# The branch between the two courses ahead of the rows' transposition, and three shared two-bank PSUM tiles

## The chip, the cores and the metric

The kernel runs on one core of one Trainium2 chip. The metric is the device time of one execution in microseconds; the median of three runs before the change is 544.16 us (542.45 to 544.39).

## The reference

Three layers follow each other. Everything is float32.

```python
scores = cap * np.tanh(scale * np.matmul(q, k.transpose(0, 1, 3, 2)) / cap)   # 2 x 12 heads, 448 x 64
attn = softmax(scores); x = (attn @ v) laid out as 896 tokens x 768
# mixture of experts: 8 experts, one for each token
expert_idx = np.argmax(logits, axis=1); gate_w = probs[np.arange(N), expert_idx]
for e in range(E):
    mask = expert_idx == e
    h = np.maximum(x[mask] @ w1[e], 0.0)          # 768 -> 1024
    out[mask] = gate_w[mask, None] * (h @ w2[e])  # 1024 -> 768
# feed-forward layer
r = np.maximum(x @ w_in, 0.0)                     # 768 -> 2048
return (s * (r * r) + b) @ w_out                  # 2048 -> 768
```

## The kernel before

The five engines each have a queue of instructions of their own: PE (matmuls), ACT, DVE and POOL (element-wise work; POOL also issues the indirect transfers) and SP (weight loads). The program runs in stages.

- **Attention**, to about 118 us, then **routing**, to about 130 us: DVE finds each token's expert and sorts the tokens by expert into slots. `rare` (L556) is a single flag made on the chip: it is 1 only where the experts' sizes don't fit the plan of two wide experts and six narrow ones. For the data that is timed it is 0.
- **Rows.** POOL gathers the sorted tokens, 128 at a time, with seven indirect transfers (L559). `rows(j)` (L652) transposes block j: six passes on PE into a PSUM tile `xt`, from which ACT copies the high part `xs0` (L668) and DVE the low part `xs1` (L669). For blocks 0 to 3 the gate is folded into the pass (L664); blocks 4 to 6 are gated on ACT first (L649) and go through a plain transposition (L662). The tiles `xt` come from the pool `ps_x`, three tiles of two banks.
- **Weights.** A matmul in float32 is made of three passes over a high and a low part (`mm3`, L638 to L641). `split` makes the parts: ACT casts the high one (L622), DVE or POOL subtracts (L623). `split1("R0", 0, pool)` and `split2("R0", 0, pool)` make the first parts of each layer, w10 and w20, with the subtraction on POOL.
- **Experts and feed-forward** are in `rest(fast)`, written once and called twice: `rest(True)` under `tc.If(rare_v < 1)` (L1044) is the fast course, `rest(False)` under `tc.If(rare_v > 0)` (L1050) the general one, with the experts' sizes in registers. Each engine loads `rare` into its sequencer (L833) and branches for itself.

Ahead of the first branch stand all seven blocks of rows, the first hidden block of the first wide expert (`layer1(0, S, 0, 0, hn)`, L710 and L712), the splits for it and for w20, and POOL's memsets (L830, L832). In `rest`, PE goes on with hidden block 1 (`hw`, L639 to L641, from w11) and the first sums `y` (from w20 and hh0), and then with the narrow experts, whose tokens DVE adds up at L771.

The sums stand in six PSUM tiles of one bank each (`accs`, tags y0 to y5, in the pool `ps_y`, which is opened after `ps_x` is closed). The last part of the feed-forward layer goes twice over half of the columns: seven sums (six tiles of `accs` and one of `ps_h`), each left by `leave(p, j)`, in which ACT (j even, L685) or DVE (j odd, L687) copies it and POOL stores it (L1011). At the end of the first half each sum gets three more passes and is left; at the end of the second half nine passes and is left. SP, PE, ACT and DVE go here in the order of the code.

Between tiles the framework sets semaphores: a write waits for what reads the tile that it overwrites, by tile. At an `If`, an engine that doesn't run a course raises the semaphores by what that course would have added; SP does this for the queues of the weight loads, after a wait for the loads that it has already issued, and POOL for the gathers.

Of the kernel before, what the change touches and what calls it, by code (L numbers as in the profile page):

```python
# [9 lines left out]
F32 = mybir.dt.float32  # L10
# [6 lines left out]
PSUM = bass.MemoryType.PSUM  # L17
# [4 lines left out]
B, H, S, D = 2, 12, 448, 64  # L22
NT = B * S
# [16 lines left out]
KD = DM // 128  # L40
NS = NT // 128
NPAD = NT + 224
# [17 lines left out]
def tile_kernel(ctx, tc, qk, vp, emb, scal, wp, wi, wo, out, dbg=None):  # L60
    nc = tc.nc
    pe, dve, act, pool, sp = nc.tensor, nc.vector, nc.scalar, nc.gpsimd, nc.sync
# [44 lines left out]
    def tabv(row, r, hi, engines=CORE):  # L107
        return nc.values_load(tab[0:1, row, r:r + 1], engines=engines, min_val=0, max_val=hi,
                              skip_runtime_bounds_check_because="made on chip from counts of tokens and one-hot rows")
# [17 lines left out]
    def done(*keys):  # L127
        for key in keys:
            used[key] = len(used)
# [25 lines left out]
    for i in range(1, 2 * NF1 + 1):  # L155
        c = i % 2
# [320 lines left out]
    xs = [big.tile([128, KD, NPAD], F32R, tag=f"a{i}", name=f"xs{i}") for i in range(2)]  # L477
# [3 lines left out]
    xctx2 = ExitStack()  # L481
    ps_x = xctx2.enter_context(tc.tile_pool(name="ps_x", bufs=3, space=PSUM, reuse_waits="tile"))
# [16 lines left out]
    def warm(n):  # L499

        t = ps_x.tile([128, 2, 512], F32, tag="xt", name="warm")
        for _ in range(n):
            pe.matmul(out=t[:, 0, 0:128], lhsT=ident, rhs=ident)
# [80 lines left out]
    dve.tensor_tensor(out=rv[:, 0], in0=rm, in1=bc(iota8[0:1], E, 1), op=ALU.mult)  # L584
    dve.tensor_reduce(out=gs, in_=gv.rearrange("p k j -> p j k"), axis=AX.X, op=ALU.add)

    warm(6)

    dgs = const.tile([128, GATES.count("p") * 128], F32, name="dgs")
    dg = {j: dgs[:, j * 128:(j + 1) * 128] for j in range(NS) if GATES[j] == "p"}  # L590
# [30 lines left out]
    def split(src, w, lo=dve):  # L621
        act.copy(out=w[0], in_=src)  # L622
        lo.tensor_tensor(out=w[1], in0=src, in1=w[0], op=ALU.subtract)  # L623

    def split1(u, f, lo=dve):
        key = (u, 0, f // 2)
        src = raw_t[key].rearrange("p (q k c j) -> p c k q j", q=4, k=KD, c=2)[:, f % 2]
        split(src, [t.rearrange("p k (q j) -> p k q j", q=4) for t in W1[f % 2]], lo)
        if f % 2:
            done(key)  # L630

    def split2(u, f, lo=dve):
        key = (u, 1, f // 2)
        split(raw_t[key].rearrange("p (c k f) -> p c k f", c=2, k=KD)[:, f % 2], W2[f % 2], lo)
        if f % 2:
            done(key)

    def mm3(out, ah, al, bh, bl, start, stop, **kw):  # L638
        pe.matmul(out=out, lhsT=ah, rhs=bh, start=start, stop=False, **kw)  # L639
        pe.matmul(out=out, lhsT=ah, rhs=bl, start=False, stop=False, **kw)  # L640
        pe.matmul(out=out, lhsT=al, rhs=bh, start=False, stop=stop, **kw)  # L641

    pump()
    rows_in.clear()
    split1("R0", 0, pool)

    def gate(j):
        if j < NS and GATES[j] == "a":
            act.mul(out=xg_t[j], in_=xg_t[j], mul=gs[:, j:j + 1])  # L649

    def rows(j):
        xg = xg_t[j]  # L652
        cs = slice(j * 128, (j + 1) * 128)

        n = 1 if j != 3 else 2
        ts = [ps_x.tile([128, 2, 512], F32, tag="xt", name="xt")[:, 0:2 // n, 0:384].rearrange("p a (k c) -> p a k c", k=3)
              for _ in range(n)]
        for kd in range(KD):
            o = ts[kd * n // KD][:, kd // 3 if n == 1 else 0, kd % 3]
            xr = xg[:, kd * 128:(kd + 1) * 128]  # L660
            if GATES[j] != "p":
                pe.transpose(out=o, in_=xr, identity=ident)  # L662
            else:
                pe.matmul(out=o, lhsT=xr, rhs=dg[j])  # L664
        for a, t in enumerate(ts):
            ks = slice(a * KD // n, (a + 1) * KD // n)
            xh, xl = (xs[i][:, ks, cs].rearrange("p (a k) c -> p a k c", k=3) for i in range(2))
            act.copy(out=xh, in_=t)  # L668
            dve.tensor_tensor(out=xl, in0=t, in1=xh, op=ALU.subtract)  # L669

    gate(0)
    gate(1)
    for j in range(4):
        if j < 2:
            gate(j + 2)
        rows(j)

    for j in range(4, NS):
        gate(j)
    hw = ps_h.tile([128, 512], F32, tag="h0", name="hw")  # L680
    hn = ps_h.tile([128, 512], F32, tag="h1", name="hn")

# [5 lines left out]


    def accs():  # L690
        return [ps_y.tile([128, 512], F32, tag=f"y{k}", name=f"y{k}") for k in range(KD)]

    def at(o, n):
        return slice(o, o + n) if isinstance(o, int) else bass.ds(o, n)

    def within(o, low):
        if isinstance(o, int):
            return o
        return nc.s_assert_within(o, 0, NT - low - 1, skip_runtime_bounds_check_because="the expert has more tokens here")

    def layer1(f, n, low, o, hw=hw):


        o = within(o, low)
        wh, wl = W1[f % 2]
        if f == 0 and hw is hn:

            for k in range(KD):
                for w in (wh, wl):
                    pe.matmul(out=hw[:, 0:n], lhsT=w[:, k], rhs=xs[0][:, k, at(o, n)], start=(k == 0 and w is wh), stop=False)  # L710
            for k in range(KD):
                pe.matmul(out=hw[:, 0:n], lhsT=wh[:, k], rhs=xs[1][:, k, at(o, n)], start=False, stop=(k == KD - 1))  # L712
        else:
            for k in range(KD):
                mm3(hw[:, 0:n], wh[:, k], wl[:, k], xs[0][:, k, at(o, n)], xs[1][:, k, at(o, n)], k == 0, k == KD - 1)
        hh, hl = (t[:, 0:n] for t in H2[f % 2])
        act.activation(out=hh, in_=hw[:, 0:n], func=ACTF.Relu)
        dve.scalar_tensor_tensor(out=hl, in0=hw[:, 0:n], scalar=0.0, in1=hh, op0=ALU.max, op1=ALU.subtract)
# [99 lines left out]


    y = [t.rearrange("p (k t) -> p k t", k=KD // 2) for t in (mem_y[:, 0:KD // 2 * NPAD], mem_y[:, KD // 2 * NPAD:])]  # L820

    split1("R0", 1)
    split2("R0", 0, pool)
    layer1(0, S, 0, 0, hn)
    for j in range(4, NS):
        rows(j)
    xctx2.close()
    ps_y = ctx.enter_context(tc.tile_pool(name="ps_y", bufs=1, space=PSUM, reuse_waits="tile"))
    for t in xs:
        pool.memset(t[:, :, NT:NPAD].bitcast(F32), 0.0)  # L830
    for t in y:
        pool.memset(t, 0.0)  # L832
    rare_v = nc.values_load(rare, engines=[ENG.SP, ENG.Pool] + CORE, min_val=0, max_val=1,  # L833
                            skip_runtime_bounds_check_because="made on chip by a comparison")
    last_ty = []

    def rest(fast):

        acc = accs()
        for s in range(1, 2 * NF1):  # L840
            f = s % NF1
# [61 lines left out]
        else:  # L903
# [3 lines left out]
            for r in range(E):  # L907
                n = tabv(2, r, NT, allc)
# [108 lines left out]
        for n in range(2 * NF):  # L1017
            p, f = divmod(n, NF)
# [22 lines left out]

    begun = [(d, d.copy()) for d in (held, used, ev, raw_t, tys)]
    to_load = loads.copy()
    with tc.If(rare_v < 1):  # L1044
        rest(True)
    for d, was in begun:
        d.clear()
        d.update(was)
    loads[:] = to_load
    with tc.If(rare_v > 0):  # L1050
        rest(False)


_OUT = (NT, DM)
# [50 lines left out]
```

## Time and profile before

| | us |
|---|---|
| median of three runs | 544.16 |
| profiled execution, its own time | 543.53 |
| span of its trace | 541.8 |
| PE busy | 515.1 (95%) |
| DVE busy | 330.0 (61%) |
| ACT busy | 231.7 (43%) |
| POOL busy | 43.5 (8%) |
| mean granted TensorE clock | 0.987 of full speed |

The page gives for each engine its busy time within the span, and then the chain of work that ended last. Around the span lie 1.73 us. A timeline names start and length of each instruction and, in brackets, how long the engine stood idle before it and what ended that. [...]

### The profile page before, as it was taken

The numbers are of one execution on the slowest core, as the hardware profiler recorded it, in microseconds if no ns is written. First come the engines' busy times: TensorE is split into PE (matmuls) and PEld (weight loads), VectorE is DVE, ScalarE is ACT, GpSimd is POOL, SyncE is SP. The second block draws the span as 40 slices with busy tenths as digits, with TensorE's granted clock in tenths as the row PEclk, the third lists the DMA queues.
The fourth block names the chain that finished last, engine by engine and source line by source line (L and its number), as shares of the span: only waits on it lengthen the run. The fifth ranks groups of instructions, "written<-read, shape, count | busy, mean of one in ns | idle before, by whom it ended". The sixth has DMA issues, their size and how long they took to land.

```text
span 541.8 us, 7919 instructions
## 1 busy us (share of the span) xinstructions
PE 515.1 (95%) x3136; PEld 418.1 (77%) x3136; DVE 330.0 (61%) x461; ACT 231.7 (43%) x318; POOL 43.5 (8%) x49
## 2 busy tenths in 40 slices
PE   6999998968899999999999899999999999999994
PEld 2344343447788888878888799999999999999994
DVE  2887788875642232432454976666668677887741
ACT  7888987852822221422134422222125333354330
POOL 2000000006430000000001100000000000150013
PEclk9999999988899999999999999999999999999998
DMA  5232542935979699879975133333223233320002
GB/s 174 106 112 58 179 126 54 421 99 189 321 230 376 209 404 365 341 250 406 389 274 197 58 124 110 118 116 117 94 93 113 110 117 116 117 105 1 2 15 92
DMA packets 30365, 93.42 MB, mean 172 GB/s; under 512 B 2376, under 2 KB 16008, under 8 KB 30320
## 3 DMA queue, kind: packets, MB, share of 16 engines
q1 hardware_dynamic: 28816, 87.30, 45.9%
q0 software_dynamic: 1488, 5.51, 2.9%
q8 instruction: 26, 0.43, 0.3%
q14 instruction: 19, 0.16, 0.1%
q10 hardware_dynamic: 16, 0.02, 0.0%
HBM read 87.32 MB, written 5.51 MB: 171 GB/s over the span
## 4 chain that ended last, share of the span: by engine, by line
PE 76%; issue 10%; ACT 5%; DVE 4%; POOL 2%; DMA 2%; POOLq 0%; ACTq 0%; DVEq 0%
PE hw L639 8%; PE hw L640 7%; PE hw L641 7%; PE y L641 6%; PE y L639 6%; PE y L640 6%; PE o L280 4%; PE s L239 4%; PE hn L639 3%; PE hn L640 3%; PE hn L641 3%; PE hn L795 3%; PE hn L779 3%; POOL out_dram L1011 2%; PE s L241 2%
## 5 line engine op out<-in xcount | busy, mean ns | idle before, releaser
L244 ACT ACTIVATE ew<-s,fscale 128x896 f32<-128x896 f32 (+1 forms) x48 | 41.7, 910 | 14.6 <-PE s L239 13.0
L949 ACT ACTIVATE xs<-mem,sc 128x896 fp32r<-128x896 f32 x31 | 32.4, 1044 | 21.5 <-PE y L640 10.5
L969 DVE SCALAR_TENSOR_TENSOR mem<-scr,sc 128x448 f32<-128x448 f32 x32 | 21.6, 681 | 32.2 <-ACT scr L968 32.2
L239 PE MATMUL s<-mem 64*128 64x448 f32 x144 | 36.3, 610 | 5.1 <-DMA mem<-in_qk_dram 4.3
L248 ACT ACTIVATE ew<-ew,sc 128x1792 f32<-128x1792 f32 (+1 forms) x24 | 38.4, 1601 | 0.8
L950 DVE SCALAR_TENSOR_TENSOR xs<-mem,sc,xs 128x896 fp32r<-128x896 f32 x31 | 34.4, 1146 | 3.1 <-ACT xs L949 1.6
L270 DVE RECIPROCAL ew<-su 128x448 f32<-128x448 f32 x12 | 35.4, 2951 | 1.1 <-PE su L266 1.1
L639 PE MATMUL hw<-xs,w11h 128*128 128x448 f32 x90 | 33.8, 375 | 0.0
L239 PEld LDWEIGHTS s<-mem 64*128 64x128 f32 x144 | 12.8, 200 | 26.9 <-issue 11.2
L640 PE MATMUL hw<-xs,w11h 128*128 128x448 f32 x90 | 33.0, 366 | 0.0
L641 PE MATMUL hw<-xs,w11l 128*128 128x448 f32 x90 | 32.9, 365 | 0.0
L280 PE MATMUL o<-ew,mem 128*64 128x448 f32 x144 | 29.7, 547 | 3.3 <-ACT sq L314 1.9
L640 PE MATMUL y<-w21l,xs 128*128 128x384 f32 x96 | 32.5, 338 | 0.0
L639 PE MATMUL y<-w21h,xs 128*128 128x384 f32 x96 | 32.5, 338 | 0.0
L641 PE MATMUL y<-w21h,xs 128*128 128x384 f32 x96 | 32.5, 338 | 0.0
L639 PE MATMUL hw<-xs,w10h 128*128 128x448 f32 x84 | 31.4, 374 | 0.0
L810 DVE SCALAR_TENSOR_TENSOR wc<-rawa,wc 128x768 int32<-128x768 int32 x32 | 30.7, 959 | 1.1
L809 DVE SCALAR_TENSOR_TENSOR wc<-rawa,wc 128x768 int32<-128x768 int32 x32 | 30.7, 959 | 1.1
L640 PE MATMUL hw<-xs,w10h 128*128 128x448 f32 x84 | 30.8, 366 | 0.0
L641 PE MATMUL hw<-xs,w10l 128*128 128x448 f32 x84 | 30.7, 365 | 0.0
L641 PE MATMUL y<-w20h,xs 128*128 128x384 f32 x90 | 30.5, 338 | 0.0
L639 PE MATMUL y<-w20h,xs 128*128 128x384 f32 x90 | 30.5, 338 | 0.0
(299 smaller groups left out, 1205.2 us busy)
## 6 DMA issues: line engine op xcount, KB each, us to landing
rawa<-in_wp_dram SPq DMA_DIRECT2D x32, 768.0 KB, 8.2
mem<-in_wp_dram SPq DMA_DIRECT2D x32, 768.0 KB, 8.6
rawa<-in_wi_dram SPq DMA_DIRECT2D x16, 768.0 KB, 4.9
rawa<-in_wo_dram SPq DMA_DIRECT2D x16, 768.0 KB, 4.3
mem<-in_qk_dram SPq DMA_DIRECT2D x12, 480.0 KB, 3.5
mem<-in_vp_dram SPq DMA_DIRECT2D x12, 256.0 KB, 3.8
xd<-x SPq DMA_DIRECT2D x2, 896.0 KB, 5.0
xd<-x SPq DMA_DIRECT2D x1, 448.0 KB
```

The lines of the kernel that those rows point to most:

```text
L239: pe.matmul(out=s[:, i, 0:S], lhsT=kq[ps, kc], rhs=kq[ps, KC:], start=True, stop=True)
L244: act.activation(out=weights(g)[:, 2 * u:2 * u + n], in_=s[:, 0:n, 0:S], func=ACTF.Tanh, scale=fscale[:, 0:1])
L248: act.activation(out=e, in_=e, func=ACTF.Exp, scale=sc[:, 0:1])
L270: dve.reciprocal(out=rs_room(g), in_=su_t.pop(g))
L280: pe.matmul(out=o[64 * i:64 * i + 64], lhsT=v[:, i * 192 + u * 64:i * 192 + u * 64 + 64], rhs=e[:, 2 * u + i], start=(u == 0), stop=False, ...
L639: pe.matmul(out=out, lhsT=ah, rhs=bh, start=start, stop=False, **kw)
L640: pe.matmul(out=out, lhsT=ah, rhs=bl, start=False, stop=False, **kw)
L641: pe.matmul(out=out, lhsT=al, rhs=bh, start=False, stop=stop, **kw)
L809: dve.scalar_tensor_tensor(out=o, in0=hi, scalar=-0x40000000, in1=o, op0=ALU.bitwise_and, op1=ALU.bitwise_or)
L810: dve.scalar_tensor_tensor(out=o, in0=lo, scalar=29, in1=o, op0=ALU.logical_shift_right, op1=ALU.bitwise_or)
L949: act.activation(out=hh, in_=h[:, f, ns], func=ACTF.Identity, bias=sc[:, 3:4])
L950: dve.scalar_tensor_tensor(out=hl, in0=h[:, f, ns], scalar=sc[:, 3:4], in1=hh, op0=ALU.add, op1=ALU.subtract)
```

## The change

1. The loads of `rare` and the branch stand ahead of the transposition of the rows. Blocks 0 to 6, the first hidden block, its splits and POOL's memsets go into `rest`, and so into both courses.
2. The general course comes first in the code. On this data each engine jumps over it, and after it falls into the fast course; before, each engine fell into the fast course and jumped over the general one at the end.
3. `warm(6)`, twelve passes that computed nothing behind the gates' matmuls `gv` (L581), is gone.
4. The subtraction of w10 goes from POOL to DVE.
5. `xt` and the sums share three tiles of two banks. `accs` gives six sums as the halves of three tiles y0, y1, y2; block j of the rows uses the tile that `at` names.

```diff
@@ routing
-    warm(6)
@@ first part of w10
-    split1("R0", 0, pool)
+    split1("R0", 0)
@@ rows(j)
-        ts = [ps_x.tile([128, 2, 512], F32, tag="xt", name="xt")[:, 0:2 // n, 0:384].rearrange("p a (k c) -> p a k c", k=3)
-              for _ in range(n)]
+        at = {0: (0,), 1: (1,), 2: (2,), 3: (0, 1), 4: (2,), 5: (0,), 6: (1,)}[j]
+        ts = [ps_y.tile([128, 2, 512], F32, tag=f"y{i}", name="xt")[:, 0:2 // n, 0:384].rearrange("p a (k c) -> p a k c", k=3)
+              for i in at]
@@ behind rows(j): the calls of gate and rows go into rest
+    xctx2.close()
+    ps_y = ctx.enter_context(tc.tile_pool(name="ps_y", bufs=1, space=PSUM, reuse_waits="tile"))
@@ accs()
-        return [ps_y.tile([128, 512], F32, tag=f"y{k}", name=f"y{k}") for k in range(KD)]
+        pairs = [ps_y.tile([128, 2, 512], F32, tag=f"y{k}", name=f"y{k}") for k in range(KD // 2)]
+        return [pairs[k // 2][:, k % 2] for k in range(KD)]
@@ ahead of rest, with the same lines removed: splits, layer1, rows 4 to 6, memsets
     rare_v = nc.values_load(rare, engines=[ENG.SP, ENG.Pool] + CORE, min_val=0, max_val=1,
                             skip_runtime_bounds_check_because="made on chip by a comparison")
     def rest(fast):
+        gate(0)
+        gate(1)
+        for j in range(4):
+            if j < 2:
+                gate(j + 2)
+            rows(j)
+        for j in range(4, NS):
+            gate(j)
+        split1("R0", 1)
+        split2("R0", 0, pool)
+        layer1(0, S, 0, 0, hn)
+        for j in range(4, NS):
+            rows(j)
+        for t in xs:
+            pool.memset(t[:, :, NT:NPAD].bitcast(F32), 0.0)
+        for t in y:
+            pool.memset(t, 0.0)
         acc = accs()
@@ the two courses
-    with tc.If(rare_v < 1):
-        rest(True)
+    with tc.If(rare_v > 0):
+        rest(False)
...
-    with tc.If(rare_v > 0):
-        rest(False)
+    with tc.If(rare_v < 1):
+        rest(True)
```

What stands in PE's queue behind the gates' matmuls (`gv`), before the change:

```order
L581 MATMUL gv_856<-ag_855,cm_800 128x21
L503 MATMUL warm_881<-ident_73 128x128 x6
L664 MATMUL xt_934<-dgs_888,mem_94 128x128 [waits DMASW1_49,DVE_49,PE_49]
L664 MATMUL xt_934<-dgs_888,mem_94 128x128 x5
L664 MATMUL xt_943<-dgs_888,mem_94 128x128 [waits DMASW2_49,DVE_49,PE_49]
```

Now, with the branch in the place of the twelve passes; a name in brackets is a semaphore that the instruction waits on:

```order
L581 MATMUL gv<-ag,cm 128x21
L815 TENSOR_LOAD rare [waits DVE_49]
L1045 COMPARE_AND_BRANCH
L664 MATMUL xt<-dgs,mem 128x128 [waits DMASW1_49,DVE_49,PE_49]
L664 MATMUL xt<-dgs,mem 128x128 x5
```

The two rows of L664 in this list are those of the general course. On this data PE goes on some 6,300 rows further down, past the raising of its semaphores, at the fast course:

```order
L1045 UNCONDITIONAL_BRANCH
L1045 UNCONDITIONAL_BRANCH [waits PE_49,PE_sequencer_49]
L1051 COMPARE_AND_BRANCH
L664 MATMUL xt<-dgs,mem 128x128 [waits DVE_49,PE_49,DMASW1_49,Activation_49,Pool_49]
L664 MATMUL xt<-dgs,mem 128x128 x5
```

The first pass over block 0 now also waits on ACT's and POOL's semaphores.

SP before, ahead of and behind its branch (in_wp are the experts' weights):

```order
L140 ISA
L140 DMA mem_94<-in_wp_dram 128x4x384 [waits DMAHW1_49]
L833 TENSOR_LOAD rare_89
L1044 COMPARE_AND_BRANCH
L143 ISA
L143 DMA rawa_93<-in_wp_dram 128x1536 [waits DVE_49,DMAHW2_49,Activation_49,Pool_49]
```

SP now, at the end of the general course, where the jump arrives, with the first load of the fast course behind it:

```order
L1045 UNCONDITIONAL_BRANCH [waits SP_sequencer_49,DMAHW0_49,DMAHW1_49,DMAHW2_49,DMAHW3_49,DMAHW4_49,DMAHW5_49,DMAHW6_49,DMAHW7_49]
L1051 COMPARE_AND_BRANCH
L143 ISA
L143 DMA rawa<-in_wp_dram 128x1536 [waits DMAHW0_49,DMAHW2_49,DVE_49,PE_49]
L143 ISA
L143 DMA rawa<-in_wp_dram 128x1536 [waits DMAHW4_49,DMAHW3_49,DMAHW6_49,DVE_49,Pool_49]
```

The loads behind the branch (L143) now stand behind a row that waits on all eight queues of the weight loads.

ACT before, from the gating of blocks 4 to 6:

```order
L649 ACTIVATE mem_94<-mem_94,gs_77 128x768 [waits DMAHW2_49,DMAHW5_49,DMASW5_49,DVE_49]
L649 ACTIVATE mem_94<-mem_94,gs_77 128x768 [waits DMAHW7_49,DMAHW2_49,DMASW6_49]
L649 ACTIVATE mem_94<-mem_94,gs_77 128x768 [waits DMASW7_49]
L622 CAST w11h_907<-rawa_93 128x768 [waits DMAHW0_49]
L622 CAST w20h_909<-rawa_93 128x768 [waits DMAHW4_49]
L717 ACTIVATE hh0h_915<-hn_977 128x448 [waits PE_49,Activation_49]
L668 CAST xs0_739<-xt_1002 128x6x128 [waits PE_49]
```

ACT now, the same place in the fast course:

```order
L648 ACTIVATE mem_94<-mem_94,gs_77 128x768 [waits DMAHW5_49,DMAHW2_49,DMASW5_49]
L648 ACTIVATE mem_94<-mem_94,gs_77 128x768 [waits DMAHW7_49,DMAHW2_49,DMASW6_49]
L648 ACTIVATE mem_94<-mem_94,gs_77 128x768 [waits DMASW7_49,DMASW0_49]
L621 CAST w11h_900<-rawa_93 128x768 [waits DMAHW0_49]
L621 CAST w20h_902<-rawa_93 128x768 [waits DMAHW6_49,DMAHW4_49]
L711 ACTIVATE hh0h_908<-hn_932 128x448 [waits PE_49]
L668 CAST xs0_739<-xt_7617 128x6x128 [waits PE_49]
```

The cast of w20h (L621 now, L622 before) waits on two queues of loads, where it waited on one.

PE before, near the end of the program, where one sum of the last half is done (nine passes) and the next one begins, here y2 and y3:

```order
L639 MATMUL y2_2986<-w21h_911,xs0_739 128x384
L640 MATMUL y2_2986<-w21l_912,xs0_739 128x384
L641 MATMUL y2_2986<-w21h_911,xs0_739 128x384
L639 MATMUL y3_2987<-w20h_909,xs0_739 128x384
L640 MATMUL y3_2987<-w20l_910,xs0_739 128x384
L641 MATMUL y3_2987<-w20h_909,xs0_739 128x384
```

PE now, the same two sums, which are the halves of the tile y1:

```order
L638 MATMUL y1_9582<-w21h_904,xs0_739 128x384
L639 MATMUL y1_9582<-w21l_905,xs0_739 128x384
L640 MATMUL y1_9582<-w21h_904,xs0_739 128x384
L638 MATMUL y1_9582<-w20h_902,xs0_739 128x384 [waits DVE_49]
L639 MATMUL y1_9582<-w20l_903,xs0_739 128x384
L640 MATMUL y1_9582<-w20h_902,xs0_739 128x384
```

The first pass into the second half now waits on DVE.

## Rows read from the trace of the kernel before

**Rows 1.** the first part of the page: busy time, share, instructions of each engine

```profile
PE 515.1 (95%) x3136; PEld 418.1 (77%) x3136; DVE 330.0 (61%) x461; ACT 231.7 (43%) x318; POOL 43.5 (8%) x49
```

**Rows 2.** timeline of PE, 124 to 154 us: start, length, engine, line, tiles

```profile
127.80 0.35 PE L581 MATMUL gv<-ag,cm 112*128 112x21 bf16 x8 [1.13 <-DVE ag L579]
...
129.50 1.58 PE L664 MATMUL xt<-dgs,mem 128*128 128x128 f32 x12
...
137.36 1.94 PE L664 MATMUL xt<-dgs,mem 128*128 128x128 f32 x12 [2.95 <-DVE xs L669]
138.96 0.72 PE L710 MATMUL hn<-xs,w10h 128*128 128x448 f32 x1
...
146.12 0.45 PE L639 MATMUL hw<-xs,w11h 128*128 128x448 f32 x1
...
149.88 0.36 PE L639 MATMUL y<-hh0h,w20h 128*128 128x448 f32 x1
```

**Rows 3.** timeline of ACT, 124 to 152 us

```profile
135.52 2.20 ACT L668 CAST xs<-xt 128x768 fp32r<-128x768 f32 x3 [9.66 <-PE xt L664]
...
142.93 0.83 ACT L622 CAST w20h<-rawa 128x768 fp32r<-128x768 f32 x1
144.50 0.55 ACT L717 ACTIVATE hh0h<-hn 128x448 fp32r<-128x448 f32 x1 [0.73 <-PE hn L712]
145.09 2.21 ACT L668 CAST xs<-xt 128x768 fp32r<-128x768 f32 x3
```

**Rows 4.** timeline of DVE, 124 to 152 us

```profile
130.04 0.41 DVE L600 TENSOR_REDUCE tab<-rv 1x32 int32<-1x256 f32 x1
...
145.93 2.69 DVE L669 TENSOR_TENSOR xs<-xt,xs 128x768 fp32r<-128x768 f32 x3 [0.23 <-ACT xs L668]
```

**Rows 5.** timeline of POOL, 124 to 152 us

```profile
133.24 0.95 POOL L559 DMA_INDIRECT mem<-xd,idx  x1 [0.30 <-issue]
...
143.84 1.88 POOL L623 TENSOR_TENSOR w20l<-rawa,w20h 128x768 fp32r<-128x768 f32 x1 [7.83 <-ACT w20h L622]
```

**Rows 6.** windows: busy time of PE, PEld, DVE, ACT, POOL, granted clock, DMA share

```profile
118.00:120.00 2.00, 1.88 (x18) 1.88 (x18) 0.94 (x5) 1.94 (x5) 0.00 (x0) 0.60 0.40 98
...
140.00:142.00 2.00, 2.00 (x7) 1.78 (x6) 0.41 (x1) 2.00 (x3) 0.00 (x0) 0.50 1.01 350
```

**Rows 7.** line L1050: each instruction, duration in ns, first and last start

```profile
L1050 SPq EVENT_SEMAPHORE  x9: 3/14/17, 475.8 to 477.0; - x9
L1050 POOLq EVENT_SEMAPHORE  x5: 17/43/43, 535.2 to 538.4; - x5
...
L1050 DVEq EVENT_SEMAPHORE  x2: 21/21/21, 538.3 to 538.5; - x2
L1050 SPq COMPARE_BRANCH  x1: 50/50/50, 471.4 to 471.4; - x1
...
L1050 DVEq COMPARE_BRANCH  x1: 69/69/69, 534.7 to 534.7; - x1
L1050 POOLq COMPARE_BRANCH  x1: 50/50/50, 535.0 to 535.0; - x1
```

**Rows 8.** line L833, the loads of rare into the sequencers

```profile
L833 DVEq TENSOR_LOAD <-rare x1: 550/550/550, 147.3 to 147.3; - x1
```

**Rows 9.** line L140, 134 to 139 us: four weight loads on SP

```profile
L140 SPq DMA_DIRECT2D mem<-in_wp_dram x4: 417/562/883, 135.0 to 137.2; - x4
...
DMA to landing us min/median/max: 6.0/7.6/11.1
```

**Rows 10.** timelines of PE and ACT, 468 to 480 us

```profile
470.56 0.34 PE L639 MATMUL y<-w21h,xs 128*128 128x384 f32 x1
...
470.76 0.48 ACT L685 COPY mem<-y 128x384 f32<-128x384 f32 x1 [2.46 <-PE y L641]
```

**Rows 11.** timelines of PE, 524 to 529 us, and DVE, 518 to 536 us

```profile
526.12 0.34 PE L639 MATMUL y<-w20h,xs 128*128 128x384 f32 x1
...
526.32 0.56 DVE L687 COPY mem<-y 128x384 f32<-128x384 f32 x1 [2.10 <-PE y L641]
```

More of the change, by code (lines that the diff above doesn't have):

```diff
@@ L669, in rows @@
             dve.tensor_tensor(out=xl, in0=t, in1=xh, op=ALU.subtract)
[L671 to L679, printed above, removed]
+    xctx2.close()
+    ps_y = ctx.enter_context(tc.tile_pool(name="ps_y", bufs=1, space=PSUM, reuse_waits="tile"))
     hw = ps_h.tile([128, 512], F32, tag="h0", name="hw")
@@ L820, in tile_kernel @@
     y = [t.rearrange("p (k t) -> p k t", k=KD // 2) for t in (mem_y[:, 0:KD // 2 * NPAD], mem_y[:, KD // 2 * NPAD:])]
[L822 to L832, printed above, removed]
     rare_v = nc.values_load(rare, engines=[ENG.SP, ENG.Pool] + CORE, min_val=0, max_val=1,
```

## The prediction

> **What bounds the kernel now.** I read the busy times first: PE works 515.1 of 541.8 us [rows 1], so whatever holds PE back is paid in full, and a change elsewhere counts only where PE waits for it. Then the timelines of PE, ACT, DVE and POOL where routing ends, since the branch moves there. PE has transposed rows from 129.50, but ACT's first copy begins at 135.52, after 9.66 us idle, PE resumes with block 3 at 137.36, after 2.95 us in which it waited for DVE, and the first hidden block begins at 138.96 [rows 2, 3]. From `hw` at 146.12 over the sums `y` at 149.88 PE runs without a gap [rows 2]. So this place has about 6 us between the first row's passes and their first use, and ACT's 135.52 is what a later start must not exceed. Why ACT began only then I can't derive: the passes on block 0 were over at 131.08 by the record. Last I read the two ends of the feed-forward layer, where sums leave their tiles: there PE doesn't wait at all [rows 10, 11].
>
> **The branch on PE, DVE and POOL.** The one jump over a whole course in the trace is at the end. DVE branches at 534.7 and its next instruction is at 538.3; SP branches at 471.4 and goes on at 475.8; POOL, whose course is short, branches at 535.0 and goes on at 535.2 [rows 7]. So 3.6 to 4.4 us for a long jump, 0.2 for POOL. After the change all of them stand ahead of the first row's passes, because the first pass waits on PE's, DVE's, ACT's and POOL's semaphores, which are raised behind the jump. DVE ends `tab` at 130.45 [rows 4], loads `rare` in 0.55 [rows 8], jumps in 3.6: 134.7. If the load waits for the subtraction of w10 too, which now stands there, it is 0.9 more (the same form takes 2.69 / 3 = 0.90 for the rows [rows 4]). POOL ends its last gather at 134.19 [rows 5], then loads and jumps: 134.9 at the least. PE's last work ahead of it, the gates' matmuls, ends at 128.15 [rows 2] and ACT's lies earlier, so their jumps end before. The first pass goes from 129.50 to about 135.1, 5.6 us later.
>
> What that costs. PE then needs 1.58 us for block 0, so ACT begins at 136.7 instead of 135.52: 1.2 late. With the clock at full speed the rest follows at PE's pace, the first hidden block begins near 140.4 instead of 138.96, and it runs at full speed, where before it fell into a stretch at 0.50 [rows 6]; these two about cancel, and `hw` starts near 146.1 again: nothing lost. The other end: PE now has nothing to do from 128.15 to 135.1, since the twelve passes are gone. Before, PE stood idle for 2.95 us ahead of 137.36, and the granted clock was 0.50 from 140 to 142 [rows 2, 6]; from 118 to 120, on the way into routing, it was 0.60. [...] Block 0 then takes about 1.4 us more (as long again as its 1.58, less the latency), blocks 1 and 2 together twice that, of which the hidden block gives some back at full speed: `hw` near 149.6, 3.5 us lost. I take the low clock as the likelier.
>
> **The branch on SP.** Here a second delay ends later. SP issued four weight loads from 135.0 to 137.2, the slowest landing 11.1 us after its issue [rows 9], so at 148.3. Behind its jump SP waits for the loads already issued, queue by queue, before it raises each queue's count. ACT's cast of w20h waits on two of the later queues. It may run when SP has passed 148.3 and six more raisings; nine of them took 1.2 us at the end [rows 7], so 0.8: 149.1. Before, the cast ran at 142.93 [rows 3]. Queued behind it on ACT are hh0h (0.55) and the copies of blocks 4 to 6 (2.21 for three) [rows 3]; w20h ends at 149.9, hh0h at 150.4, the copy of block 5 at 151.9, DVE's subtraction for it, with 0.90 apiece, at 153.0. The first sum y0 uses the tile of block 5, so PE begins `y` at about 153.1 instead of 149.88: 3.2 us. Below: if the loads land a little sooner, as SP's next one no longer competes with them from 144.2, 1.5; above: 4.0. POOL's subtraction for w20 (1.88 [rows 5]) ends at 151.9 and hides behind this. The two delays don't add; the later one counts, 3.2 or 3.5. I take 3.3 for the front, 1.5 to 6 with another microsecond or two for instruction fetches under the traffic of the gathers.
>
> [...]
>
> **The sums in pairs.** This is the largest term. A tile is now two sums, and a write waits for the readers of the tile. At the end of the second half PE finishes sum j in nine passes, DVE copies it, and the next sum is in the other half of the same tile: its first pass now waits for that copy. In the trace the next sum starts at 526.12, while the copy runs from 526.32 to 526.88 [rows 11]. With some 0.05 us for the semaphore PE starts at 526.93: 0.81 lost, three times (three tiles), 2.4, and up to 0.12 more each because the pipeline has run empty: 2.4 to 2.8. At the end of the first half it is ACT's copy, 470.76 to 471.24, where the next sum began at 470.56 [rows 10]: 0.73, three times, 2.2 to 2.5. PE is in order and has nothing else there, so all of it counts: 4.6 to 5.3; I take 4.9. Elsewhere the pairs cost nothing: between the two wide experts a hidden block lies between the copies and the next sums, and it covers them.
>
> **The end, and the rest.** Removing the jump at the end gains little: DVE's goes on at 538.3, when POOL, which waits there for the last stores, has its last event at 538.4 [rows 7]. I take 0.1, up to 0.6 if POOL's own work there falls away. The weight split on DVE in place of POOL, and `warm`, cost nothing beyond what is counted. SP's next loads come some 4 us later, as does PE, so they hide as before.
>
> Sum against the profiled execution (543.53): 543.53 + 3.3 + 4.9 - 0.1 = 551.6. That execution lies 0.6 below the median of 544.16, so I forecast 551.8, between the two.
>
> **Rivals.**
> - *The front costs nothing, or gives back.* The early branch falls into the 9.66 us in which ACT stood idle; ACT's 135.52 is set by the gathers' traffic anyway, the loads land in time, and the hidden block runs at full speed, which gains up to 2.2 us with the tail. For it: the idle time is there. Against it: SP's wait for 148.3 is later than anything in before's order. 543.5 + 4.9 - 2.2 = 546.2. That is not slower by more than 0.5%, or 2.7 us (546.9 from the median), which is about what a measurement of this kernel can tell from no change. It decides if w20h is cast before about 146. 12%.
> - *The front is dearer.* Jumps under the gathers' traffic take 2 us more, or POOL's is a long one (3.6 instead of 0.2, the first pass at 138.5), and the clock stays low. 543.5 + 7 + 4.9 = 555.4. 17%.
> - *The pairs don't bind*: the change doesn't make the waits cost what I say, for instance because the copy overlaps the next sum's weight load. Then 543.5 + 3.3 = 546.9, half of it on either side of the bound. 6%.
> - *Faster*: the first and the third together. 541.5. 2%.
>
> **How the numbers follow.** The forecast has 63%, its own range 549.8 to 553.5. The range that holds 8 in 10 takes in most of the dearer front and, at its lower end, half of the two cases about 546.5: 546.5 to 555.6. Slower by over 0.5%: 63 + 17 + 3 + 3 (the free front with dearer pairs) = 86%; faster 2%; within 12%.
>
> **What would show it.** In the changed profile: first rows' passes near 135 and a gap of 3.5 us behind the branch on PE, ACT and DVE; a granted clock of 0.50 about there; w20h cast near 149 and `y` near 153; six gaps of 0.7 to 0.9 us on PE, three near the middle of the sums and three near the end, each ended by a copy from `y`. The forecast is wrong if w20h is cast before 146, or if PE runs through those six places without a gap.

## The result and the profile after

The changed kernel takes 550.40 us (median of 6 runs, 549.83 to 550.87); the kernel before takes 543.08 us in the runs beside it. The ratio is 1.0118, with a 95% interval of 1.0089 to 1.0146: slower by 1.2%. The forecast was 551.8 us, in a range of 546.5 to 555.6.

The page of the changed kernel begins with the span and with the busy times, which answer to [rows 1]:

```profile
span 549.1 us, 7928 instructions
...
PE 515.2 (94%) x3124; PEld 416.4 (76%) x3124; DVE 330.9 (60%) x462; ACT 231.7 (42%) x318; POOL 40.5 (7%) x48
```

PE does the same work (515.2 us busy, 515.1 before) in a span that is 7.3 us longer. So it was made to wait. The waits by what ended them, of PE in the changed kernel (engine, line, what it waited for: total us, times, the longest), are these; none of the five rows stands in the kernel before:

```profile
PE xt L664 <- DVEq L1045: 6.8, 1, 6.8
...
PE y L638 <- DVE mem L680: 2.0, 3, 0.7
...
PE y L638 <- DVE xs L669: 1.7, 1, 1.7
...
PE y L638 <- ACT mem L678: 1.1, 2, 0.6
...
PE y L638 <- ACT scr L678: 0.6, 1, 0.6
```

The first row is the jump, the third is what lies behind SP's wait, and the second, fourth and fifth are the sums in pairs. The timeline of PE at the first two places, which answers to [rows 2], from the gates' matmuls `gv` on:

```profile
128.77 0.35 PE L581 MATMUL gv<-ag,cm 112*128 112x21 bf16 x8 [1.27 <-DVE ag L579]
135.88 7.17 PE L664 MATMUL xt<-dgs,mem 128*128 128x128 f32 x48 [6.76 <-DVEq L1045]
...
148.53 0.45 PE L638 MATMUL hw<-xs,w11h 128*128 128x448 f32 x1
...
154.13 0.47 PE L638 MATMUL y<-hh0h,w20h 128*128 128x448 f32 x1 [1.67 <-DVE xs L669]
```

The first pass over the rows begins 7.1 us behind the start of `gv`, where it was 1.7 (129.50 behind 127.80), and `y` 25.4 us behind it, where it was 22.1. The branches, at line L1045 (duration in ns, first and last start), answer to [rows 7]:

```profile
L1045 SPq EVENT_SEMAPHORE  x9: 17/17/17, 145.6 to 150.2; - x9
L1045 POOLq EVENT_SEMAPHORE  x5: 17/42/43, 130.4 to 139.4; - x5
...
L1045 DVEq EVENT_SEMAPHORE  x2: 21/21/21, 135.6 to 135.7; - x2
...
L1045 PEldq COMPARE_BRANCH  x1: 4787/4787/4787, 129.4 to 129.4; - x1
L1045 POOLq COMPARE_BRANCH  x1: 53/53/53, 129.9 to 129.9; - x1
L1045 DVEq COMPARE_BRANCH  x1: 72/72/72, 131.9 to 131.9; - x1
...
L1045 SPq COMPARE_BRANCH  x1: 50/50/50, 139.7 to 139.7; - x1
```

An engine's branch and its first event behind it are the two ends of its jump: 131.9 to 135.6 on DVE, 129.9 to 130.4 on POOL. PE's own branch is recorded with its jump, 4.8 us. SP's nine events span 145.6 to 150.2. ACT, with idle time and what ended it in brackets, answers to [rows 3]:

```profile
138.96 0.80 ACT L668 CAST xs<-xt 128x768 fp32r<-128x768 f32 x1 [12.23 <-PE xt L664]
...
146.88 0.83 ACT L621 CAST w11h<-rawa 128x768 fp32r<-128x768 f32 x1 [0.77 <-SPq L1045]
150.25 0.83 ACT L621 CAST w20h<-rawa 128x768 fp32r<-128x768 f32 x1 [2.54 <-SPq L1045]
```

Both casts were released by SP's line L1045, the second at 150.25. In the last part of the feed-forward layer, where [rows 10, 11] show PE without a gap, it now waits; three of the six places, in PE's timeline:

```profile
475.69 0.44 PE L638 MATMUL y<-w21h,xs 128*128 128x384 f32 x1 [0.57 <-ACT mem L678]
...
479.46 0.45 PE L638 MATMUL y<-w21h,xs 128*128 128x384 f32 x1 [0.57 <-ACT scr L678]
...
537.88 0.44 PE L638 MATMUL y<-w20h,xs 128*128 128x384 f32 x1 [0.65 <-DVE mem L680]
```

The end is shorter. The last store, before and then after:

```profile
535.11 0.97 POOL L1011 DMA_INDIRECT out_dram<-mem,idx  x1 [0.75 <-DVE mem L687]
```

```profile
544.76 0.97 POOL L1012 DMA_INDIRECT out_dram<-mem,idx  x1 [1.66 <-DVE mem L680]
```

The program ends at 549.1, 4.34 us behind the issue of this store, where it was 6.69 (535.11 to 541.8). The closing line of the program, before and then after (L1101 and L1102, the same line):

```profile
L1101 POOLq DRAIN  x3: 46/103/1869, 539.1 to 541.5; - x3
```

```profile
L1102 POOLq DRAIN  x3: 40/109/3624, 544.7 to 548.9; - x3
```

A drain is an instruction of the program's end; the three durations are the shortest, the median and the longest, in ns. Before, the long one of 1.9 us began at 539.1, behind the events with which POOL closed the jumped course (535.2 to 538.4 [rows 7]; in that trace a store lands 3.4 us after its issue). Now the long one of 3.6 us starts at 544.7, while the last store is still on its way: its packets move from 546.2 to 547.0.

Put together, by the starts of the same instructions in the two traces:

| place | before | after | later by | added in this stretch |
|---|---|---|---|---|
| gates' matmuls `gv` (code unchanged ahead of them) | 127.80 | 128.77 | 0.97 | 0.97 |
| first sum `y` | 149.88 | 154.13 | 4.25 | 3.28 |
| first pass of the second half of the sums | 473.74 | 480.62 | 6.88 | 2.63 |
| last matmul | 533.74 | 543.40 | 9.66 | 2.78 |
| end of the span | 541.8 | 549.1 | 7.3 | -2.36 |

The two rows behind `y` in PE's timeline, before and then after:

```profile
473.74 0.34 PE L639 MATMUL hn<-w20h,xs 128*128 128x384 f32 x1
...
533.74 0.34 PE L641 MATMUL y<-w21h,xs 128*128 128x384 f32 x1
```

```profile
480.62 0.34 PE L638 MATMUL hn<-w20h,xs 128*128 128x384 f32 x1
...
543.40 0.33 PE L640 MATMUL y<-w21h,xs 128*128 128x384 f32 x1
```

The first row of the table is the start of the program, not the change: in the thirteen traces of this study `gv` begins anywhere between 127.18 and 128.77. Without that row the table gives 6.3 us, while the medians differ by 7.3 (by 6.7 to 7.1 with the medians of before that stand beside the experiments). The difference is not explained.

### The profile page after: what moved, and what is told of

It is laid out like the page before. It is cut to its first block, busy times and chain, and to the rows that moved or that the text cites. A ratio compares the mean times of both kernels' runs of the same rounds, so it can differ in the third digit from the quotient of the medians.

```text
span 549.1 us, 7928 instructions
## 1 busy us (share of the span) xinstructions
PE 515.2 (94%) x3124; PEld 416.4 (76%) x3124; DVE 330.9 (60%) x462; ACT 231.7 (42%) x318; POOL 40.5 (7%) x48
## 4 chain that ended last, share of the span: by engine, by line
PE 56%; issue 10%; POOL 2%; DVE 1%; ACT 1%; POOLq 0%; ACTq 0%
PE hw L638 7%; PE hw L639 7%; PE hw L640 7%; PE y L638 6%; PE y L640 6%; PE y L639 6%; PE hn L638 3%; PE hn L639 3%; PE hn L640 3%; PE hn L789 3%; PE hn L773 3%; POOL out_dram L1012 2%; ACT xs L881 1%; DVE mem L680 0%; DVE xs L669 0%
## 5 line engine op out<-in xcount | busy, mean ns | idle before, releaser
L950 ACT ACTIVATE xs<-mem,sc 128x896 fp32r<-128x896 f32 x31 | 32.4, 1044 | 21.5 <-PE y L639 11.0
L970 DVE SCALAR_TENSOR_TENSOR mem<-scr,sc 128x448 f32<-128x448 f32 x32 | 21.7, 682 | 32.2 <-ACT scr L969 32.2
L638 PE MATMUL y<-w20h,xs 128*128 128x384 f32 x90 | 30.8, 342 | 2.0 <-DVE mem L680 2.0
L639 PE MATMUL y<-w20l,xs 128*128 128x384 f32 x90 | 30.5, 338 | 0.0
```

What stands on the lines that cost most here:

```text
L950: act.activation(out=hh, in_=h[:, f, ns], func=ACTF.Identity, bias=sc[:, 3:4])
```

## The experiments

Each was timed beside the kernel before on the same chip; medians of before lie between 543.3 and 543.7 in all of them. "Behind `gv`" is measured from the start of the gates' matmuls, to leave the program's start out.

**Sums apart.** The six sums are taken in another order, so that two in a row never share a tile.

```diff
         banks = accs()
+        banks = banks[0::2] + banks[1::2]
```

> The changed kernel, but the feed-forward layer's last part takes the six sums in the order first halves, then second halves of the three tiles, so that two sums that follow each other never share a tile. Theory of the pairs (each next sum waits for the copy of its tile's other half; measured in the changed kernel as six gaps and 2.48 + 2.77 us against the kernel before): the six gaps of PE, 0.57 to 0.65 us each, go; the time falls by 5.0 to 5.3 us to about 545.2. Rival (the copies themselves or the stores are the bound there, and the gaps only move): within 0.5 us of 550.4.

Measured: 544.66 us, ratio to before 1.0016 (1.0003 to 1.0029). 5.7 us less than the changed kernel. PE's timeline at the place where the changed kernel had its first three waits:

```profile
476.03 0.34 PE L640 MATMUL y<-w21h,xs 128*128 128x384 f32 x1
476.44 0.44 PE L638 MATMUL y<-w21h,xs 128*128 128x384 f32 x1
...
478.11 0.34 PE L638 MATMUL hn<-w20h,xs 128*128 128x384 f32 x1
...
537.20 0.34 PE L640 MATMUL y<-w21h,xs 128*128 128x384 f32 x1
```

No bracket is left; the largest step between two passes here, from 476.03 to 476.44, is one of 0.41 us where the usual one is 0.18. The time between `y` and the first pass of the second half falls from 326.49 to 324.33 us, and from there to the last matmul from 62.78 to 59.09. So the waits of the pairs are removed by an order alone, the tiles still shared. But 59.09 is also less than the 60.00 us of the kernel before: through the second half PE's passes now start about every 0.173 us and no longer every 0.177, in all five traces with the sums apart. So some 0.9 of the 5.7 us isn't the waits. Why the passes come closer together is not shown, and this order was not tried in the kernel before.

**Casts ahead of the branch.** The part "h" of a split is ACT's cast, "l" the subtraction.

```diff
     split1("R0", 0)
+    split1("R0", 1, part="h")
+    split2("R0", 0, part="h")
...
-        split1("R0", 1)
-        split2("R0", 0, pool)
+        split1("R0", 1, part="l")
+        split2("R0", 0, pool, part="l")
```

> The changed kernel, but ACT's two casts w11h and w20h stand ahead of the branch; their subtractions stay in the courses. Theory of SP's wait (y starts at 154.1 because the cast of w20h, and with it hh0h and the copies of blocks 4 to 6, waits for SP's raising of the load counts behind 149.4): hh0h near 148, y starts when hw ends and POOL's w20l is done, near 152.3; 1.8 us faster, 548.6. Rival (the late start of the rows on PE sets y, SP's wait is hidden): y within 0.3 us of 154.1, 550.4.

Measured: 548.58 us, ratio 1.0090 (1.0076 to 1.0103). The time is as expected; the trace shows less. ACT's timeline, then PE's:

```profile
126.38 0.83 ACT L622 CAST w20h<-rawa 128x768 fp32r<-128x768 f32 x1
...
147.24 0.54 ACT L716 ACTIVATE hh0h<-hn 128x448 fp32r<-128x448 f32 x1 [0.83 <-PE hn L711]
```

```profile
135.07 8.27 PE L669 MATMUL xt<-dgs,mem 128*128 128x128 f32 x48 [6.64 <-DVEq L1050]
...
148.92 0.45 PE L641 MATMUL hw<-xs,w11h 128*128 128x448 f32 x1
...
152.68 0.36 PE L641 MATMUL y<-hh0h,w20h 128*128 128x448 f32 x1
```

The cast of w20h is at 126.38 and hh0h at 147.24, so SP's wait is off the path, and PE goes from `hw` into `y` without a pause. But `hw` itself begins 20.8 us behind `gv`, where it was 19.8 in the changed kernel, and `y` 24.6 behind it, where it was 25.4: 0.8 us earlier. That `hw` is later isn't this edit's doing. The 48 passes over the first rows take 8.27 us here and 7.17 in the changed kernel's trace, where the granted clock is 0.50 from 136 to 138 and 0.78 from 138 to 140 (that it rose later here is my estimate from the two lengths); in two runs that leave the casts where they were (the sums apart, and warm(6) put back, below) they take 8.12 and 8.21, and there PE's wait ahead of `y` is 0.7 us or less, not 1.67. So SP's wait and the late rows end close together, and how long the passes over the rows take decides what SP's wait costs: `y` comes 25.0 to 25.7 us behind `gv` in four traces with the wait, and 24.4 and 24.6 in two without. The rest of the difference between the two profiled executions (549.27 and 550.87) is mainly the start of the program (`gv` at 128.09 against 128.77).

**Fast course first**, the branch still early.

```diff
-    with tc.If(rare_v > 0):
-        rest(False)
+    with tc.If(rare_v < 1):
+        rest(True)
...
-    with tc.If(rare_v < 1):
-        rest(True)
+    with tc.If(rare_v > 0):
+        rest(False)
```

> The changed kernel with the fast course first in the code and the general one second, as before the change: the early branch falls through, the long jump is at the end again. Theory (front cost is the long jump and SP's wait behind it, 3.3 us; the tail is 2.35 us shorter because POOL and SP no longer go through the skipped course's end): first rows' passes near 130.5, y near 150, tail as before; 3.3 less and 2.35 more: 549.5. Rival A (the early branch costs by its place, taken or not): front unchanged, tail longer: 552.8. Rival B (the shorter tail has nothing to do with the order of the courses): 547.1.

Measured: 545.98 us, ratio 1.0054 (1.0032 to 1.0075), faster than any of the three expectations. The end is long again, 7.8 us behind the last store's issue, so the short end does belong to the order of the courses. At the front PE's passes begin early, as expected, but ACT's first copy comes earlier than in the kernel before. PE's timeline, then ACT's:

```profile
128.05 0.35 PE L581 MATMUL gv<-ag,cm 112*128 112x21 bf16 x8 [0.34 <-DVE ag L579]
129.72 7.59 PE L664 MATMUL xt<-dgs,mem 128*128 128x128 f32 x48 [1.31 <-DMA mem<-xd,idx]
```

```profile
132.97 0.80 ACT L668 CAST xs<-xt 128x768 fp32r<-128x768 f32 x1 [7.27 <-PE xt L664]
```

`y` is 18.6 us behind `gv`, 6.8 less than in the changed kernel and 3.5 less than in the kernel before. So the jump, with SP's wait behind it, costs 6.8 here, and something else in the change gains some 3 us: the runs on warm(6), below.

**Courses exchanged in the kernel before**, nothing else: the branch stays behind the rows.

```diff
-    with tc.If(rare_v < 1):
-        rest(True)
+    with tc.If(rare_v > 0):
+        rest(False)
...
-    with tc.If(rare_v > 0):
-        rest(False)
+    with tc.If(rare_v < 1):
+        rest(True)
```

> The kernel before, with only the order of the two courses in the code exchanged: the branch stays behind the seven blocks, the long jump is there and no longer at the end. Theory: PE's jump of 4 to 5 us begins near 145 while its matmuls run to 146.1, so PE resumes near 149.5, 3.5 us late, with SP's wait inside that; the tail is 2.35 us shorter; together 1 to 2.5 us slower than before, about 545. Rival (the shorter tail came from the early branch or the shared tiles): 546.5 to 547.

Measured: 548.78 us, ratio 1.0090 (1.0074 to 1.0107), 5.2 slower than before where 1 to 2.5 was expected. The end is 4.35 us, as in the changed kernel: that part held, and here neither the early branch nor the shared tiles can have done it. The front was mis-sized. PE's timeline, and line L1044:

```profile
150.92 0.71 PE L639 MATMUL hw<-xs,w11h 128*128 128x448 f32 x1 [4.94 <-DVEq L1044]
...
154.70 0.47 PE L640 MATMUL hw<-xs,w11h 128*128 128x448 f32 x1 [0.83 <-POOLq L1044]
```

```profile
L1044 POOLq EVENT_SEMAPHORE  x5: 17/43/43, 154.6 to 155.0; - x5
...
L1044 DVEq COMPARE_BRANCH  x1: 72/72/72, 147.9 to 147.9; - x1
```

I had counted PE's own jump. PE waits for DVE's, which branches only at 147.9, behind its subtractions for the rows, and then once more for POOL, which raises its semaphore at 154.6, behind its memsets; the passes of `hw` in between take 0.57 us each, those behind it 0.37. In the kernel before, the hidden block's passes take 0.57 where the granted clock is 0.50 (140 to 142), and 0.37 from 142.4. `y` is 29.4 us behind `gv` (22.1 before): 7.3 more, less 2.3 at the end, is the 5.

**Best of both orders: fast course first, sums apart.** Both edits above on the changed kernel.

> The changed kernel with the fast course first (as in the run before) and the six sums in the order first halves, then second halves. If the two effects stand side by side (fast course first: y 6.8 us earlier after the gates' matmuls than in the changed kernel; sums apart: 5.25 us less), 545.98 - 5.2 = 540.8, faster than both kernels. Rival (the gain of the early front is given back at the end, where the stores bound the tail): 543.

Measured: 540.86 us, ratio 0.9963 (0.9934 to 0.9993): faster than both kernels.

**The same with warm(6) put back.**

```diff
     dve.tensor_reduce(out=gs, in_=gv.rearrange("p k j -> p j k"), axis=AX.X, op=ALU.add)
 
+    warm(6)
```

> The run with the fast course first and the sums apart, with the twelve passes of warm(6) put back behind the gates' matmuls. In the kernel before, ACT's first copy of the rows began at 135.5, in the run with the fast course first at 133.0. Theory W (warm(6) holds up PE's semaphore for block 0; in the kernel before warm's own update comes at 131.2, 1.6 us behind its recorded end): ACT's first copy back at about 135.5, y 3 us later, 543.8. Theory B (the delay came from the branch's place or from POOL's subtraction): ACT's first copy stays near 133, and the time within 0.7 us of the run without warm.

Measured: 542.04 us, ratio 0.9978 (0.9952 to 1.0005), against 540.86 without: the two intervals overlap, so the times alone don't part them. In the traces, one of each, ACT's first copy does. With warm:

```profile
135.86 2.20 ACT L669 CAST xs<-xt 128x768 fp32r<-128x768 f32 x3 [9.69 <-PE xt L665]
```

Without it (fast course first, sums apart) it began at 132.33. `y` comes 20.6 us behind `gv` with warm and 19.7 without; that is less sure, since the run with the fast course first alone, with the same front, has 18.6. The granted clock doesn't explain it, since it goes the other way: here is the stretch 132 to 134 with warm, then without (PE, PEld, DVE, ACT, POOL busy, granted clock, DMA share, GB/s):

```profile
132.00:134.00 2.00, 1.02 (x9) 1.02 (x10) 0.00 (x0) 0.00 (x0) 1.39 (x3) 1.00 0.77 250
```

```profile
132.00:134.00 2.00, 2.00 (x11) 2.00 (x11) 0.84 (x1) 0.80 (x1) 1.39 (x3) 0.50 0.81 257
```

With warm the granted clock stayed at 1.00; without, it was at 0.50 here, and the kernel was still not slower.

**The same with the subtraction of w10 on POOL.**

```diff
-    split1("R0", 0)
+    split1("R0", 0, pool)
```

> The run with the fast course first and the sums apart, with the subtraction of w10 put back on POOL. Theory P (POOL's subtraction from 134.2 to 136.0 held up the copies of the rows in the kernel before): ACT's first copy back near 135.5, about 3 us slower. Rival: ACT's first copy stays near 133; POOL's branch comes behind the subtraction, 1.8 us later, but on the path only where PE waits for POOL, so within 0.5 us of the run without it.

Measured: 541.01 us, ratio 0.9975 (0.9948 to 1.0003). ACT's first copy comes 6.3 us behind `gv` (133.76), which is 2.1 later than without the edit, but `y` stays at 19.7 and the time doesn't move. So this subtraction on POOL is not what costs the time; the next run, which keeps it, has the first copy at 4.85.

**The kernel before without warm(6).**

```diff
-    warm(6)
```

> The kernel before without the twelve passes of warm(6), nothing else. Theory W: ACT's first copy near 133, 2 to 3 us faster than before, about 541. Rival (the delay has another cause, and the longer pause of PE lowers the clock for the rows): ACT's first copy at 135.5 or later, within 0.5 us of before or up to 1.5 us slower.

Measured: 541.27 us, ratio 0.9963 (0.9938 to 0.9987). ACT's timeline:

```profile
133.06 0.80 ACT L667 CAST xs<-xt 128x768 fp32r<-128x768 f32 x1 [6.74 <-PE xt L663]
135.97 1.88 ACT L667 CAST xs<-xt 128x768 fp32r<-128x768 f32 x3 [2.10 <-PE xt L663]
```

The first copy comes 4.85 us behind `gv`, where it was 7.72 before; `y` 19.7 behind it, where it was 22.1. One line taken away gains 2.0 us by the ratio and 2.4 at `y`, as much as the best of the other versions: the early branch and the shared tiles add nothing to it that these times show. PE's timeline tells where the 2.4 us lie:

```profile
138.50 0.45 PE L709 MATMUL hn<-xs,w10h 128*128 128x448 f32 x1
...
144.16 0.45 PE L638 MATMUL hw<-xs,w11h 128*128 128x448 f32 x1
```

The first hidden block `hn` begins 10.3 us behind `gv`, where it was 11.2: 0.9 us by the earlier copy. From `hn` to `hw` it is 5.66 us, where it was 7.16 [rows 2]: 1.5 us by the clock, which is 1.00 from 140 to 142 here and was 0.50 [rows 6]. With warm(6) PE kept its clock through the first rows (1.00 from 128 to 138), then waited 2.95 us for the late copies [rows 2], and the clock fell over the hidden block. In the run with the fast course first, the sums apart and warm(6) the clock didn't fall there (1.00 from 138 to 144), and warm(6) cost only 0.9 us at `y`. These parts are read from one execution of each; the times show their sum.

**The changed kernel with warm(6) put back.**

> The changed kernel with the twelve passes of warm(6) put back behind the gates' matmuls, ahead of the branch. In the kernel before, taking warm out alone gave 2.3 us. Theory (in the changed kernel PE has to wait for DVE's jump until about 7 us behind the gates' matmuls and y waits for SP, so warm's passes lie in idle time): y within 0.5 us of 25.4 us behind the gates' matmuls, 550.4 within 0.7. Rival (warm delays the rows here too): y 2 us later, 552.5.

Measured: 549.87 us, ratio 1.0118 (1.0094 to 1.0142), the ratio of the changed kernel. First pass over the rows 7.25 us behind `gv` (7.11 without), `y` 25.0 (25.4). Ahead of the jump, warm's passes cost nothing and their removal gains nothing.

**The changed kernel with the subtraction of w10 on POOL.**

> The changed kernel with the subtraction of w10 put back on POOL, behind the gathers and ahead of POOL's branch. PE's first pass over the rows waits on POOL's semaphore, which is raised behind POOL's own work. Theory (that wait is on the path and DVE's jump and POOL's work end at about the same time): first pass about 1.5 us later, at 8.6 us behind the gates' matmuls, y 1 to 1.5 us later, 551.5. Rival (DVE's jump, now without the subtraction ahead of it, sets the start): first pass 0 to 0.9 us earlier, 550.

Measured: 550.11 us, ratio 1.0113 (1.0087 to 1.0139), no change. PE's timeline:

```profile
135.99 7.32 PE L664 MATMUL xt<-dgs,mem 128*128 128x128 f32 x48 [7.95 <-POOLq L1045]
...
153.31 0.47 PE L638 MATMUL y<-hh0h,w20h 128*128 128x448 f32 x1 [0.58 <-DVE xs L669]
```

The wait is there, now ended by POOL, and the first pass comes 8.3 us behind `gv`, 1.2 later, as the theory said; but `y` is 25.6 behind it (25.4 before the edit), because SP's wait ends later anyway: it releases ACT's cast of w20h at 149.43, 21.7 us behind `gv` (21.5 before the edit). So the theory's wait is right and its price is wrong.

**Casts ahead and sums apart**, the general course still first.

> The changed kernel with both the sums in the order first halves, then second halves, and the casts of w11h and w20h ahead of the branch: do the two gains add up? Measured apart they gave 5.7 and 1.8 us. If they add: 543.4 to 544, with the short tail of 4.4 us and the general course still first in the code. Rival (one eats the other's gain): 544.7 or more.

Measured: 542.54 us, ratio 0.9993 (0.9974 to 1.0013): no different from the kernel before. The two gains add up (550.4 less 5.7 and 1.8 is 542.9; the 543.4 to 544 that was expected is too high). A version with the passes over blocks 0 to 2 ahead of the branch was not tried.

## Why the prediction was right

**The sums in pairs**, forecast 4.9 us: 2.63 and 2.78, 5.4 together. The gaps are where they were put, three and three, ended by ACT's copy in the first half and DVE's in the second. The brackets, 0.57 and 0.65 us, are less than what is lost: the step into the next sum is 0.91 and 0.98 us where the usual one is 0.18, so 0.73 and 0.81 as forecast, 4.6 together, and the step behind it is 0.1 longer too (0.28). From the end of the copy to the next pass it is 0.05 us (475.64 to 475.69, 537.83 to 537.88), as put for the semaphore. The order of the sums takes the gaps away, and with them some 4.8 of the 5.7 us. This term was shown, and was slightly low.

**The front**, forecast 3.3 us: 3.28. The steps, with the late start of 0.97 us taken off: first pass forecast at 135.1, measured at 134.9; cast of w20h at 149.1, measured 149.3; `y` at 153.1, measured 153.2. The wait is ended by a subtraction of DVE (third row of the waits), by its time that for block 5, as forecast. The low clock came too; in the changed kernel, columns as above:

```profile
134.00:136.00 2.00, 0.12 (x1) 0.15 (x1) 0.00 (x0) 0.00 (x0) 1.30 (x2) 0.50 0.99 319
...
140.00:142.00 2.00, 2.00 (x21) 2.00 (x19) 1.65 (x2) 1.19 (x2) 0.00 (x0) 1.00 1.06 383
```

It is 0.50 in the pause and into the rows, and 1.00 again from 140. What the late rows cost by themselves was too high: I put `hw` at 149.6, and it came at 147.6 (148.53 less 0.97), so not 3.5 but 1.4 us later than before; in the other traces with the jump 2.3 to 2.8. I had both delays nearly equal and took the later one. That they end close together is shown by the runs: without SP's wait `y` comes 0.8 us earlier, with 1.2 us more on the rows 0.2 later. One reading didn't hold: I let POOL branch behind its last gather, at 134.9 at the least, but it branched at 129.9 with its gathers running until 135.6. DVE's jump, which I had at 134.7, set the start (134.6 less the late start), so this cost the forecast nothing.

**What was right for a smaller reason than I had.** I wrote that taking out warm(6) costs nothing beyond the clock. In the changed kernel that holds (put back, it changes nothing). In the kernel before it doesn't: there warm(6) cost 2.0 to 2.4 us, 0.9 of it at `y` by ACT's late first copy and 1.5 by the clock that fell over the hidden block. That is a part of the answer to what I could not derive, why ACT began only at 135.52: without these passes the first copy comes earlier, those of the next blocks don't. So the front's 3.3 is a net figure: with the fast course first, `y` came 2.3 and 3.5 us earlier than before (the runs with the sums apart and without), so the jump, with SP's wait, costs 5.6 to 6.8. I had its sum right from the side of what ends last, SP's wait, which covers both. My rival that the front gives something back named the wrong cause, the gathers' traffic; and it would have come true had the general course not been put first.

**The step that failed is the end.** Forecast a gain of 0.1 us, up to 0.6; measured 2.36. I compared DVE's arrival (538.3) with POOL's last event (538.4) [rows 7] and took POOL's event for the end of a wait that stays. It doesn't: by their times the waits for the stores are part of closing the jumped course, and what follows them, POOL's drain of 1.9 us, did not begin before (539.1). With nothing jumped, the drain starts under the last store (at 544.7; the store is issued at 544.76). Exchanging the courses in the kernel before alone shows it: 6.69 to 4.35 us.

The sum made against the profiled execution was 543.53 + 3.3 + 4.9 - 0.1 = 551.6. Measured: 543.5 + 1.0 (start of the program) + 3.3 + 5.4 - 2.4 = 550.8, the profiled execution's own time being 550.87. That the two totals lie 0.8 apart is partly luck: the late start, which isn't the change, and the dearer pairs make up for much of what the end gained. In the rivals 543.5 + 3.3 is 546.8 and 543.5 - 2.2 is 541.3, which moves no bound. The rivals fall: the front didn't give back (12%), the pairs did bind (6%), the front was not dearer (17%).

The front's range had a microsecond or two for instruction fetches under the traffic of the gathers; no run shows this term. What they show in its place: DVE's jump, which set the start, took 3.7 us in the changed kernel with a DMA share of 0.89, under the gathers, and 3.6 at the end of the kernel before [rows 7] with one of 0.36. PE's took 4.8 and 3.7, but ended first in the changed kernel, at 134.2; POOL's short one took 0.5. What an engine does during a long jump is not shown, and that the distance decides was not tested apart.

## What to carry to other kernels

Put first in the code the course that the data takes (545.98 us here, against 550.40 with the other one first); where the jump must come, look for a place where every engine of the next step idles (no run here found one). What counts is the last of the engines' jumps (DVE's, 131.9 to 135.6) and of the waits that close the jumped course (SP's, to 150.2), which include transfers in flight that nobody needs yet. Before two accumulators are put into one tile, look at the order in which they are left; if neighbours share a tile, each next one waits for the copy of the last, 0.57 to 0.65 us each here. And try the removal of passes that only keep TensorE awake, one at a time: here one group of them held the clock for the rows (1.00 from 130 to 134, against 0.56 and 0.58 without it), and the kernel was faster without it (ratio 0.9963).

## What I had not expected of the hardware

- **Passes that only keep the clock up delayed later work.** Taking out twelve passes behind `gv` in the kernel before moves ACT's first copy from 7.72 to 4.85 us behind `gv`; in the version with the fast course first and the sums apart it is at 4.23 without them and at 7.81 with them. By the records the passes over block 0 were done at 131.08 in the kernel before, 4.4 us ahead of the copy that waited for them, and ACT then copied three blocks without a further wait [rows 3], so the later blocks' signals were there as well. Ends of matmuls are modelled in such a record, so it may be PE's work or its signal that was late; which of them, and why, stays open.
- **A clock held for the rows could still fall behind them.** In the version with the fast course first and the sums apart, warm(6) kept the granted clock at 1.00 through the rows and behind them; without it the clock fell to 0.50 (132 to 134), after a pause of PE behind `gv`, and `y` still came 0.9 us earlier. In the kernel before, with warm(6), the clock fell to 0.50 later, over the hidden block (140 to 142), behind a wait of PE of 2.95 us, and that cost 1.5 us.
- **The end of the program depends on the jumped course.** 4.3 to 4.4 us from the last store's issue to the end where the course that ran is the last in the code, 6.6 to 7.8 us where another one is jumped behind it.
